# Converting the second layer's other half of the weights beside that layer instead of ahead of it, and rounding g on ScalarE

## The chip, the core and the metric

The kernel runs on one core of a Trainium2 chip. A core has a matrix engine (TensorE, PE in the rows), a vector engine (VectorE, DVE), an activation engine (ScalarE, ACT), a general engine (GpSimd, POOL) and a queue engine (SyncE, SP) that issues all of this kernel's transfers between memory (DRAM) and the on-chip buffer. The metric is the device time of one execution in microseconds (us). TensorE has two clock levels, 1.2 and 2.4 GHz; the profile tells which share of full speed was granted.

## The reference

Attention with a memory term gives x of 2304 tokens by 512. Two feed-forward layers follow, each with a hidden width of 2048 and an activation of its own:

```python
def _moe_ref(x, w_in, w_out):
    h = x @ w_in                      # (2304,512) @ (512,2048)
    g = h * np.cos(h)
    return g @ w_out                  # (2304,2048) @ (2048,512)

def _moe2_ref(x, w_in, w_out):
    h = x @ w_in
    sp = log1p(exp(min(h, 20)))       # softplus
    g = h * np.tanh(sp)               # "mish"
    return g @ w_out
```

All weights arrive as 64-bit floats, 8 bytes a number. The kernel has to turn them into 32-bit numbers itself, and it splits every matmul operand into a rounded part (H) and a remainder (L), so that each product is made of three matmuls: H with H, H with L, L with H.

## The kernel before, in words

Four stretches follow each other. **Stage A** is attention over 16 (batch, head pair) steps, with the first half of the first layer (hidden columns 0 to 1023, called `m1`) woven in. **Stage B** is what is left of `m1`, while the weights of the first layer's second half are converted. **Stage C** is the first layer's second half (`m2`): for each block of 512 tokens eight units, a unit being one group of 128 hidden columns. **Stage D** is the whole second layer (`m3`), sixteen units a block, the first eight with the weights `w_c` (first half), the other eight with `w_d` (second half).

A unit has two steps. `first` (L445) is 12 matmuls of the token block with `w_in` into a PSUM tile `h`; `second` (L503 in stages B and C, L512 in D) is 12 matmuls of g with `w_out` into `y`. The loop in `ffn` takes units in pairs: `first` of two units, then `second` of the two units before them. Between the two steps the other engines make g. In stage C (`elem_cos`): ScalarE turns h into a whole number of turns (L392), VectorE subtracts these (L393), ScalarE takes a sine over both units of the pair at once (L397), VectorE multiplies by h (L400), which is the last reader of h; then `split` rounds g (L113 to L117, on the engine that the table `TURNS` names) and subtracts the rounded part (L417, on GpSimd in stage C). In stage D (`elem_mish`): one ScalarE instruction (L409), a rounding on ScalarE, a subtraction in turn on VectorE and GpSimd.

A piece of weights (512 KB of 64-bit numbers, 128 x 512 of them; 16 pieces a half) goes through `to_f32`: a load into one of two buffers `wst` (L123), a rescaling on GpSimd (L117), one step on ScalarE (L126), three on VectorE (L127, L128, L131). `load_half` then rounds it (L113 on ScalarE or L117 on GpSimd, in turn) and subtracts (L161, VectorE or GpSimd, in turn).

In stage C of the kernel before, the 16 pieces of `w_c` go through this whole path, and then 16 pieces of `w_d` through `to_f32` alone (`convert_ahead`), and are stored to a scratch tensor `w2s` in DRAM. In stage D `from_scratch` reads them back and only the rounding and the subtraction are left to do.

The order of instructions on each engine is fixed when the program is built: a scheduler takes the instructions by their place in the program text and by a timeline of its own, and gives each buffer out again when its last reader is done. `tc.issue_after(x)` puts what follows on the engine of x behind x. On the chip each engine, and the SP queue, runs its list strictly in that order; an instruction that waits holds up all that stand behind it. `BUFS` says how many buffers a name has; `h` is a PSUM tile of one bank, `y` takes four banks.

Of the kernel before, what the change touches and what calls it, by code (L numbers as in the profile page):

```python
# [9 lines left out]
F32 = mybir.dt.float32  # L10
F32R = mybir.dt.float32r
I32 = mybir.dt.int32
# [6 lines left out]
TWO_PI = 2.0 * math.pi  # L19
BIG = 8.0e9  # L20
BUFS = dict(
    mb=2, raw=3, aD=4, kh=3, kl=3, qs=2, vt=2, qt=1, ph=2, den=2, mo=4, xH=1, xL=3, sm=7, mn=2, at=8, aT=7, u=2, e=3, g=4, h=3, y=4, xb=3, yp=3, yh=2, yl=2, wg=2, wst=2, S=6, T=8,
)
RES = 2
TOUCH = 1
# [6 lines left out]

TURNS = dict(
    sc0="p", ql0="vp", kh0="a", kl0="vp", qh0="a", aT0="a",
    sc="p", ql="vp", kh="p", kl="ppv", ws="p", w0l="pv", w1l="vp", w2l="vp", w3l="vp", gl="p", gh="v", mh="a",
    wh="ap", aT="av", yl="p", ml="vp", y0="v", y1="a", qh="a", aD="v",
)

# [5 lines left out]
def attention_moe_moe_kernel(  # L44
# [14 lines left out]
    nc = tc.nc  # L59
    P = 128  # L60
    B, NP, _, S = kT.shape
# [4 lines left out]
    TB = 256  # L66
# [43 lines left out]
    def scaled(kind, dst, src, scale=1.0, first=False):  # L110
        eng = turn_of(kind, first)
        if eng is nc.scalar:
            eng.activation(dst, src, AF.Copy, scale=scale)  # L113
        elif scale == 1.0 and eng is nc.vector:
            eng.tensor_copy(dst, src)  # L115
        else:
            eng.tensor_scalar(dst, src, scale, 1.0, ALU.mult, ALU.mult)  # L117
# [16 lines left out]
    def weight_pieces(win, wout, half, tl):  # L134

        f0 = half * FH + tl * 2 * P
        wi = win.bitcast(I32).rearrange("(c p) (f two) -> p c f two", p=P, two=2)
        for c in range(0, NC, 2):
            yield wi[:, c:c + 2, f0:f0 + 2 * P, :]
        wo = wout.bitcast(I32).rearrange("(f p) (e two) -> p f e two", p=P, two=2)  # L140
        for f in range(f0 // P, f0 // P + 2):
            yield wo[:, f]
# [22 lines left out]
    def from_double(win, wout, half):  # L165
# [1 line left out]
            for src in weight_pieces(win, wout, half, tl):  # L167
                yield to_f32(src)
        return f

    w2s = tc.dram_tile([NTL * 4, P, SM], F32, name="w2s")

    def convert_ahead():
        for tl in range(NTL):
            for n, src in enumerate(weight_pieces(w2i, w2o, 1, tl)):
                t = wk.tile([P, SM], I32, tag="wg", name="wg", bufs=BUFS["wg"])
                nc.sync.dma_start(w2s[4 * tl + n], to_f32(src, t))
                yield 0

    def from_scratch(tl):  # L180
        for n in range(0, 4, 2):
            t = wk.tile([P, 2, SM], F32, tag="u", name="wt", bufs=BUFS["u"])
            nc.sync.dma_start(t, w2s[4 * tl + n:4 * tl + n + 2].rearrange("n p f -> p n f"))
            yield t[:, 0]
            yield t[:, 1]

    def drain(g):
        for _ in g:
            pass
# [190 lines left out]
    last_sin = [None]  # L380
    marks = {}

    def elem_cos():

        state = []

        def f(h, last):
            if not state:
                state.append(wk.tile([P, 2, SM], F32, tag="u", name="u", bufs=BUFS["u"]))
            u2 = state[0]  # L390
            u = u2[:, len(state) - 1]
            nc.scalar.activation(u.bitcast(I32), h, AF.Copy, scale=INV2PI, bias=0.25)  # L392
            nc.vector.scalar_tensor_tensor(u, u.bitcast(I32), -TWO_PI, h, ALU.mult, ALU.add)  # L393
            state.append(h)
            if len(state) < 3:
                return []
            last_sin[0] = nc.scalar.activation(u2, u2, AF.Sin, bias=c_hpi).ins  # L397
            out = []
            for i in range(2):
                nc.vector.tensor_tensor(u2[:, i], state[1 + i], u2[:, i], ALU.mult)  # L400
                out.append(split(u2[:, i], "gl"))
            state.clear()
            return out
        return f

    def elem_mish():
        def f(h, last):
            e = wk.tile([P, SM], F32, tag="e", name="e", bufs=BUFS["e"])
            nc.scalar.activation(e, h, AF.Mish)  # L409
            return [split(e, "ml")]  # L410
        return f

    def split(g, kind):
        gg = wk.tile([P, 2, SM], F32R, tag="g", name="g", bufs=BUFS["g"])
        gH, gL = gg[:, 0], gg[:, 1]
        scaled("gh" if kind == "gl" else "mh", gH, g)
        turn_of(kind).tensor_tensor(gL, g, gH.bitcast(F32), ALU.subtract)  # L417
        return gH, gL

# [146 lines left out]
    def psum(name):  # L566
# [6 lines left out]
    w1p = ctx.enter_context(tc.tile_pool(name="w1p"))  # L573
    m_pools = [psum("psM")]
    at = attention(ap, [ps_a])
    m1 = ffn(m_pools, seq1, {0: w_a}, elem_cos(), load_block(xsH, xsL, True, TB), mm2_t, fin_partial,
             lambda blk: sum(blk) <= stored[0] * S)
    k_done = 0
    pieces = [0]
# [28 lines left out]
        drain(gb)  # L608
    b_pools = [psum("psB")]
    w_c, gc = load_half(w0p, "w2", from_double(w2i, w2o, 0), "w2l")  # L610
    ge = convert_ahead()
    m2 = ffn(b_pools, seq2, {1: w_b}, elem_cos(), load_block(xsH, xsL, True), mm2_t, fin_full)
    with tc.issue_after(marks["sp"]):
        for i, _ in enumerate(m2):
            if i % 2 and next(gc, 1):
                next(ge, None)
    drain(gc)
    drain(ge)
    w_d, gd = load_half(w1p, "w3", from_scratch, "w3l")
    with tc.issue_after(last_sin[0]):  # L620
        table = nc.scalar.preload_act_table_set("mish").ins
    m3 = ffn(b_pools, seq3, {0: w_c, 1: w_d}, elem_mish(), load_block(ysH, ysL, False), mm2_n, fin_out)
# [70 lines left out]
```

## Time and profile before

| | |
|---|---|
| median of 3 runs | 1109.83 us (1108.22 to 1111.08) |
| the profiled execution | 1113.66 us |
| its span, first to last instruction | 1111.9 us |
| TensorE busy | 1061.8 us, 95% |
| VectorE, ScalarE, GpSimd busy | 531.1, 450.9, 430.6 us |
| mean granted TensorE clock | 0.975 |

The profiled execution is 1.8 us longer than its span, and 3.8 us (0.3%) above the median of the runs. "Busy" for TensorE includes the time for which a matmul was held, and the ends of matmuls are modelled, so the starts of matmuls and the waits in front of them say more than the share. In the rows, L445 is line 445 of the kernel above; PE is the matmul, PEld the load of weights into the array that goes ahead of it; "x24" is 24 instructions; `u`, `e` and `g` are the tiles between `first` and `second`.

### The profile page before, as it was taken

Reading aid. Unit: us, or ns where it says so; the run is one execution under the profiler, and the core shown is the slowest. Engines: PE = TensorE matmul, PEld = TensorE weight load, DVE = VectorE, ACT = ScalarE, POOL = GpSimd, SP = SyncE. Lnnn points to the kernel's source line nnn. Section 1 sums busy time; section 2 is a strip of 40 time slices with the busy share of each in tenths; the row PEclk is TensorE's granted clock in tenths of the full one; section 3 lists DMA queues with packets and bytes.
Section 4 is the critical chain, followed back from the end, with each engine's and each line's share of the span. In section 5 each row is a group of like instructions: output and inputs, shape, how many; then the busy total and the mean of one; then the engine's idle time right before and its main releaser. Section 6 shows DMA issues by size and latency. Waiting matters only on the chain.

```text
span 1111.9 us, 17626 instructions
## 1 busy us (share of the span) xinstructions
PE 1061.8 (95%) x6672; PEld 903.1 (81%) x6672; DVE 531.1 (48%) x1282; ACT 450.9 (41%) x911; POOL 430.6 (39%) x454
## 2 busy tenths in 40 slices
PE   6988999999999999999988799999999999999998
PEld 5766788888888899987766578988888888888897
DVE  7989776557565558665777776520000000000000
ACT  6776475545454534343434333331222232131221
POOL 6987463416152334455556444670101010111100
PEclk8989799999999999999999989999999999999999
DMA  6555541414121274324565765730210210110010
GB/s 230 187 191 161 163 137 47 149 57 139 56 84 49 64 268 152 115 95 152 195 225 165 243 217 194 246 124 1 76 39 0 77 38 1 57 38 1 19 39 19
DMA packets 70853, 125.43 MB, mean 113 GB/s; under 512 B 6000, under 2 KB 25456, under 8 KB 70768
## 3 DMA queue, kind: packets, MB, share of 16 engines
q1 hardware_dynamic: 70768, 124.30, 33.8%
q8 instruction: 53, 0.87, 0.3%
q14 instruction: 32, 0.26, 0.1%
HBM read 91.77 MB, written 32.51 MB: 112 GB/s over the span
## 4 chain that ended last, share of the span: by engine, by line
PE 65%; DVE 12%; DMA 9%; ACT 6%; POOL 4%; issue 4%; SPq 0%; POOLq 0%; ACTq 0%; DVEq 0%
PE h L445 27%; PE y L512 18%; PE y L503 9%; DMA wst<-in_w2i_dram 4%; PE o L349 3%; PE tp L322 3%; PE sp L262 3%; DVE wst L127 2%; DMA wst<-in_w1i_dram 2%; DVE wst L131 2%; DVE wst L128 1%; ACT wst L126 1%; DMA wst<-in_w2o_dram 1%; DMA wst<-in_w1o_dram 1%; PE o L338 1%
## 5 line engine op out<-in xcount | busy, mean ns | idle before, releaser
L445 PE MATMUL h<-xbH,w 128*128 128x256 f32 (+1 forms) x1536 | 400.8, 341 | 15.8 <-DVE u L400 14.3
L445 PEld LDWEIGHTS h<-xbH,w 128*128 128x128 f32 x1536 | 268.9, 191 | 54.4 <-DVE u L400 18.7
L445 PE MATMUL h<-xbL,w 128*128 128x256 f32 (+1 forms) x768 | 259.8, 338 | 0.0
L503 PE MATMUL y<-g,w 128*128 128x256 f32 (+1 forms) x1344 | 227.5, 322 | 5.7 <-POOL g L417 3.9
L503 PEld LDWEIGHTS y<-g,w 128*128 128x128 f32 x1344 | 194.8, 195 | 30.7 <-POOL g L417 8.1
L512 PE MATMUL y<-w,g 128*128 128x512 f32 x864 | 201.8, 389 | 0.0
L512 PEld LDWEIGHTS y<-w,g 128*128 128x128 f32 x864 | 161.9, 188 | 33.4
L417 DVE TENSOR_TENSOR g<-e,g 128x512 fp32r<-128x512 f32 x36 | 25.6, 711 | 333.9 <-ACT g L113 333.9
L417 POOL TENSOR_TENSOR g<-e,g 128x512 fp32r<-128x512 f32 x36 | 47.0, 1305 | 313.5 <-ACT g L113 313.5
L445 PEld LDWEIGHTS h<-xbL,w 128*128 128x128 f32 x768 | 146.5, 191 | 15.1 <-issue 0.2
L409 ACT ACTIVATE e<-h 128x512 f32<-128x512 f32 x72 | 43.0, 597 | 252.1 <-PE h L445 252.1
L290 POOL TENSOR_SCALAR at<-at,sm,omg 128x128 f32<-128x128 f32 (+2 forms) x144 | 108.7, 766 | 86.6 <-DVE sm L288 51.3
L417 POOL TENSOR_TENSOR g<-u,g 128x512 fp32r<-128x512 f32 x72 | 97.9, 1373 | 88.4 <-DVE g L115 81.6
L126 ACT ACTIVATE wst<-wst,c_seven 128x512 int32<-128x512 uint32 x64 | 49.2, 769 | 110.5 <-DMA wst<-in_w2o_dram 36.8
L267 ACT ACTIVATE at<-at,mn 128x128 f32<-128x128 f32 (+3 forms) x128 | 71.0, 556 | 31.3 <-DVE mn L264 29.0
L117 POOL TENSOR_SCALAR wst<-wst 128x512 f32<-128x512 f32 x64 | 46.0, 719 | 82.8 <-DMA wst<-in_w2o_dram 21.3
L127 DVE SCALAR_TENSOR_TENSOR wst<-wst 128x512 int32<-128x512 int32 x64 | 56.5, 883 | 43.8 <-POOL wst L117 30.3
L322 PE MATMUL tp<-ident,at 128*128 128x128 f32 x384 | 67.3, 295 | 7.3 <-DVE xL L354 3.7
L349 PE MATMUL o<-aT,vt 128*64 128x128 f32 (+1 forms) x896 | 65.3, 277 | 0.0
L393 DVE SCALAR_TENSOR_TENSOR u<-u,h 128x512 f32<-128x512 int32 x72 | 48.9, 681 | 34.3 <-ACT u L392 34.2
L264 DVE CUSTOM_DVE_ANT_0 at<-sp,mask 128x128 f32<-128x128 f32 (+3 forms) x128 | 59.0, 481 | 9.3 <-PE sp L262 8.8
L322 PEld LDWEIGHTS tp<-ident,at 128*128 128x128 f32 x384 | 44.7, 147 | 20.0 <-POOL at L290 10.4
(98 smaller groups left out, 1239.5 us busy)
## 6 DMA issues: line engine op xcount, KB each, us to landing
wst<-in_w1i_dram SPq DMA_DIRECT2D x16, 512.0 KB, 3.7
wst<-in_w1o_dram SPq DMA_DIRECT2D x16, 512.0 KB, 4.3
wst<-in_w2i_dram SPq DMA_DIRECT2D x16, 512.0 KB, 4.3
wst<-in_w2o_dram SPq DMA_DIRECT2D x16, 512.0 KB, 4.9
qd<-in_qT_dram SPq DMA_DIRECT2D x16, 320.0 KB, 3.2
vt<-in_vn_dram SPq DMA_DIRECT2D x16, 320.0 KB, 3.3
xbH<-xsH SPq DMA_DIRECT2D x20, 256.0 KB, 4.5
xbL<-xsL SPq DMA_DIRECT2D x20, 256.0 KB, 4.5
```

The lines of the kernel that those rows point to most:

```text
L126: nc.scalar.activation(lo, lo.bitcast(U32), AF.Relu, scale=-(2.0 ** -29), bias=c_seven)
L127: nc.vector.scalar_tensor_tensor(lo, hi, 3, lo, ALU.logical_shift_left, ALU.bitwise_or)
L264: nc.vector.tensor_tensor_reduce(at[:, :N], sp[:, :N], mask[:, SM - q0:SM - q0 + N], SSC, 3.0e38, ALU.add, ALU.min, mn[:, j:j + 1])
L267: marks["act"] = nc.scalar.activation(at[:, :N], at[:, :N], AF.Exp, bias=mn[:, j:j + 1], scale=-1.0, accum_out=sm[:, j:j + 1]).ins
L290: turn_of("sc", b == 0).tensor_scalar(at[:, :N], at[:, :N], sm[:, j:j + 1], gates[j], ALU.mult, ALU.mult)
L322: nc.tensor.transpose(tp[:, c:c + P], at[:, c:c + P], ident)
L349: marks["pe"] = nc.tensor.matmul(o[j * D:(j + 1) * D, :n], st["vt"][:kk, c, j * D:(j + 1) * D], a, start=False, stop=c == i, skip_group_ch ...
L393: nc.vector.scalar_tensor_tensor(u, u.bitcast(I32), -TWO_PI, h, ALU.mult, ALU.add)
L417: turn_of(kind).tensor_tensor(gL, g, gH.bitcast(F32), ALU.subtract)
L445: nc.tensor.matmul(h[:, a * T:(a + 1) * T], w_[:, c, f0:f0 + P], x_[c], start=m == 0, stop=m == 3 * NC - 1)
L503: nc.tensor.matmul(y[e // per][:, cols], w_[:, f, es], g_, start=fst and m == 0 and e % per == 0, stop=lst and m == 2, skip_group_check=True)
L512: nc.tensor.matmul(y[t], g_[:, tsl], w_[:, f, :], start=fst and m == 0, stop=lst and m == 2, skip_group_check=True)
```

## The change

`convert_ahead`, `from_scratch`, the scratch tensor `w2s` and its buffers `wg` are gone. `w_d` is loaded with `from_double`, as the other three halves are, so its 16 pieces go through the whole path of `to_f32`, rounding and subtraction while stage D runs. Stage C converts `w_c` alone, one piece every fourth step of the unit loop in the program text where it was every second. In stage C the rounding of g moves from VectorE to ScalarE (`bh="a"`; stages A and B keep `gh="v"`). `h` gets a fourth buffer.

```diff
-    mb=2, ..., g=4, h=3, y=4, ..., wg=2, wst=2, S=6, T=8,
+    mb=2, ..., g=4, h=4, y=4, ..., wst=2, S=6, T=8,
...
-    ..., gl="p", gh="v", mh="a",
+    ..., gl="p", gh="v", bh="a", mh="a",
...
-    w2s = tc.dram_tile([NTL * 4, P, SM], F32, name="w2s")
-    def convert_ahead():
-        for tl in range(NTL):
-            for n, src in enumerate(weight_pieces(w2i, w2o, 1, tl)):
-                t = wk.tile([P, SM], I32, tag="wg", name="wg", bufs=BUFS["wg"])
-                nc.sync.dma_start(w2s[4 * tl + n], to_f32(src, t))
-                yield 0
-    def from_scratch(tl):
-        for n in range(0, 4, 2):
-            t = wk.tile([P, 2, SM], F32, tag="u", name="wt", bufs=BUFS["u"])
-            nc.sync.dma_start(t, w2s[4 * tl + n:4 * tl + n + 2].rearrange("n p f -> p n f"))
-            yield t[:, 0]
-            yield t[:, 1]
...
-    def elem_cos():
+    def elem_cos(cast):
...
-                out.append(split(u2[:, i], "gl"))
+                out.append(split(u2[:, i], cast, "gl"))
...
-            return [split(e, "ml")]
+            return [split(e, "mh", "ml")]
-    def split(g, kind):
+    def split(g, cast, kind):
...
-        scaled("gh" if kind == "gl" else "mh", gH, g)
+        scaled(cast, gH, g)
...
-    m1 = ffn(m_pools, seq1, {0: w_a}, elem_cos(), ...
+    m1 = ffn(m_pools, seq1, {0: w_a}, elem_cos("gh"), ...
...
-    ge = convert_ahead()
-    m2 = ffn(b_pools, seq2, {1: w_b}, elem_cos(), load_block(xsH, xsL, True), mm2_t, fin_full)
+    m2 = ffn(b_pools, seq2, {1: w_b}, elem_cos("bh"), load_block(xsH, xsL, True), mm2_t, fin_full)
     with tc.issue_after(marks["sp"]):
         for i, _ in enumerate(m2):
-            if i % 2 and next(gc, 1):
-                next(ge, None)
+            if i % 4 == 1:
+                next(gc, None)
     drain(gc)
-    drain(ge)
-    w_d, gd = load_half(w1p, "w3", from_scratch, "w3l")
+    w_d, gd = load_half(w1p, "w3", from_double(w2i, w2o, 1), "w3l")
```

Up to the start of stage C every engine's order is the same. The places that matter after it are these. The line numbers of the changed kernel are 16 lower from `from_scratch` on (L417 is L401, L540 is L524, L392 is L376, L397 is L381, L409 is L393, L537 is L521, L621 is L603).

**GpSimd in the later part of stage C.** `wst` is a weight piece, `g<-u` the subtraction of stage C, `yl` that of the result y. Before:

```order
L417 TENSOR_TENSOR g<-u,g 128x512 x2
L117 TENSOR_SCALAR wst<-wst 128x512 x3
L417 TENSOR_TENSOR g<-u,g 128x512 x2
L117 TENSOR_SCALAR wst<-wst 128x512 x2
L417 TENSOR_TENSOR g<-u,g 128x512 x2
L117 TENSOR_SCALAR wst<-wst 128x512 x4
L417 TENSOR_TENSOR g<-u,g 128x512
L540 TENSOR_TENSOR yl<-yp,yh 128x512
```

In the changed program, from the last piece of `w_c` (`w_6532`) to the first of `w_d`:

```order
L161 TENSOR_TENSOR w_6532<-wst,w_6531 128x512
L117 TENSOR_SCALAR wst<-wst 128x512 x2
L401 TENSOR_TENSOR g<-u,g 128x512 x2
L524 TENSOR_TENSOR yl<-yp,yh 128x512 x4
L401 TENSOR_TENSOR g<-u,g 128x512 x8
L524 TENSOR_TENSOR yl<-yp,yh 128x512 x4
L401 TENSOR_TENSOR g<-u,g 128x512 x8
L524 TENSOR_TENSOR yl<-yp,yh 128x512 x4
L401 TENSOR_TENSOR g<-u,g 128x512 x2
L117 TENSOR_SCALAR w_8145<-wst 128x512
```

The pieces between the g of this stretch are gone but for the two that are rescaled early (the second row): they are the first two of `w_d`, loaded into the free `wst` buffers, and the rest of their way follows in stage D.

**ScalarE where stage C ends.** `u<-u,c_hpi` is the last sine of stage C, ACT_TABLE_LOAD brings the table for mish, `e<-h` is mish. Before:

```order
L397 ACTIVATE u<-u,c_hpi 128x1024
L621 ACT_TABLE_LOAD
L113 ACTIVATE w_8290<-wt 128x512
L113 ACTIVATE w_8292<-wt 128x512
L113 ACTIVATE w_8294<-wt 128x512
L537 ACTIVATE yh<-yp 128x512
L409 ACTIVATE e<-h 128x512
```

In the changed program:

```order
L381 ACTIVATE u<-u,c_hpi 128x1024
L603 ACT_TABLE_LOAD
L126 ACTIVATE wst<-wst,c_seven 128x512 x2
L113 ACTIVATE g<-u 128x512 x2
L113 ACTIVATE w_8145<-wst 128x512
L393 ACTIVATE e<-h 128x512
L113 ACTIVATE g<-e 128x512
L126 ACTIVATE wst<-wst,c_seven 128x512 x2
L113 ACTIVATE w_8147<-wst 128x512
```

The rounding of stage C's last two g now stands behind the table load and two conversion steps, and conversion steps of `w_d` stand between the mish of the first units.

**GpSimd in stage D, where the last pieces of `w_d` are made.** `w_82..`/`w_81..` are the parts of `w_d`. Before, with `wt` the piece read back from scratch:

```order
L417 TENSOR_TENSOR g<-e,g 128x512
L161 TENSOR_TENSOR w_8299<-wt,w_8298 128x512
L117 TENSOR_SCALAR w_8300<-wt 128x512
L161 TENSOR_TENSOR w_8301<-wt,w_8300 128x512
L117 TENSOR_SCALAR w_8302<-wt 128x512
L161 TENSOR_TENSOR w_8303<-wt,w_8302 128x512
L117 TENSOR_SCALAR w_8304<-wt 128x512
L161 TENSOR_TENSOR w_8305<-wt,w_8304 128x512
L417 TENSOR_TENSOR g<-e,g 128x512 x34
```

In the changed program, the same place:

```order
L401 TENSOR_TENSOR g<-e,g 128x512
L117 TENSOR_SCALAR w_8155<-wst 128x512
L117 TENSOR_SCALAR wst<-wst 128x512
L161 TENSOR_TENSOR w_8156<-wst,w_8155 128x512
L117 TENSOR_SCALAR wst<-wst 128x512 x2
L117 TENSOR_SCALAR w_8157<-wst 128x512
L161 TENSOR_TENSOR w_8158<-wst,w_8157 128x512
L401 TENSOR_TENSOR g<-e,g 128x512
L117 TENSOR_SCALAR wst<-wst 128x512
L117 TENSOR_SCALAR w_8159<-wst 128x512
L161 TENSOR_TENSOR w_8160<-wst,w_8159 128x512
L401 TENSOR_TENSOR g<-e,g 128x512 x30
```

Two of GpSimd's g of stage D stood ahead of the last part of `w_d` before; in the changed program six do. The g in the middle of the last fence belongs to the twelfth unit of stage D and stands behind the rescaling of the first piece of the eighth and last pair of pieces (the second of the "x2").

## Rows read from the trace of the kernel before

**Rows 1.** The page: busy time and share; granted clock in 40 slices, in tenths.
```profile
PE 1061.8 (95%) x6672; PEld 903.1 (81%) x6672; DVE 531.1 (48%) x1282; ACT 450.9 (41%) x911; POOL 430.6 (39%) x454
...
PEclk8989799999999999999999989999999999999999
```

**Rows 2.** Stretches from:to us, length; busy of PE, PEld, DVE, ACT, POOL; clock, DMA share, GB/s.
```profile
483.00:600.00 117.00, 107.56 (x483) 85.50 (x483) 80.72 (x135) 42.83 (x62) 64.80 (x60) 1.00 0.49 161
600.00:720.00 120.00, 109.74 (x553) 91.73 (x552) 82.98 (x113) 40.78 (x57) 59.84 (x51) 0.97 0.68 229
720.00:1112.00 392.00, 388.30 (x1805) 325.12 (x1803) 31.46 (x44) 102.69 (x170) 64.46 (x51) 1.00 0.11 38
```

**Rows 3.** Timeline of TensorE: start us, us, engine, line, what.
```profile
483.42 0.40 PE L445 MATMUL h<-xbH,w 128*128 128x512 f32 x1
...
720.28 0.63 PE L445 MATMUL h<-xbH,w 128*128 128x512 f32 x2
```

**Rows 4.** Chain of waits in 483:720: start us, us, what.
```profile
640.70 8.33 PE h L445 x24
...
675.82 5.44 PE h L445 x24
...
686.70 5.75 PE h L445 x48
```

**Rows 5.** Waits in 483:720: who for whom, us in total, times, longest.
```profile
ACT wst L126 <- DMA wst<-in_w2o_dram: 36.8, 12, 7.4
...
ACT wst L126 <- DMA wst<-in_w2i_dram: 32.1, 14, 5.0
...
PEld h L445 <- DVE u L400: 18.7, 10, 5.9
...
PEld y L503 <- POOL g L417: 7.0, 9, 1.5
...
PEld y L503 <- DVE g L115: 2.0, 2, 1.5
```

**Rows 6.** Chain of waits in 523:548: one loop of a weight buffer.
```profile
535.71 3.38 DMA wst<-in_w2o_dram
...
539.16 0.76 ACT wst L126
539.92 0.49 ACT u L392
...
542.59 0.69 DVE wst L127
543.28 0.68 DVE wst L128 x2
543.95 0.61 DVE wst L131
...
544.64 0.66 POOL w L117
...
545.37 1.65 POOL w L161
...
547.04 3.62 DMA wst<-in_w2i_dram
```

**Rows 7.** Groups in 483:600: busy us, mean ns | idle before.
```profile
L131 DVE TENSOR_TENSOR wst<-wst 128x512 int32<-128x512 int32 x19 | 15.7, 825 | 0.1
...
L115 DVE CAST g<-u 128x512 fp32r<-128x512 f32 x20 | 8.2, 443 | 0.0
```

**Rows 8.** The same groups' view in 600:720.
```profile
L131 DVE TENSOR_TENSOR wg<-wst 128x512 int32<-128x512 int32 x15 | 16.4, 1093 | 1.5 <-POOL g L417 1.2
```

**Rows 9.** The same view in 709:820, the start of stage D.
```profile
L417 POOL TENSOR_TENSOR g<-e,g 128x512 fp32r<-128x512 f32 x10 | 13.5, 1346 | 62.9 <-ACT g L113 62.9
```

**Rows 10.** Timeline where stage C ends, ScalarE and TensorE.
```profile
707.29 1.28 ACT L621 ACT_TABLE_LOAD   x1
...
709.27 0.40 PE L445 MATMUL h<-xbH,w 128*128 128x512 f32 x1
```

More of the change, by code (lines that the diff above doesn't have):

```diff
@@ L21 @@
 BUFS = dict(
-    mb=2, raw=3, aD=4, kh=3, kl=3, qs=2, vt=2, qt=1, ph=2, den=2, mo=4, xH=1, xL=3, sm=7, mn=2, at=8, aT=7, u=2, e=3, g=4, h=3, y=4, xb=3, yp=3, yh=2, yl=2, wg=2, wst=2, S=6, T=8,
+    mb=2, raw=3, aD=4, kh=3, kl=3, qs=2, vt=2, qt=1, ph=2, den=2, mo=4, xH=1, xL=3, sm=7, mn=2, at=8, aT=7, u=2, e=3, g=4, h=4, y=4, xb=3, yp=3, yh=2, yl=2, wst=2, S=6, T=8,
 )
@@ L34 @@
     sc0="p", ql0="vp", kh0="a", kl0="vp", qh0="a", aT0="a",
-    sc="p", ql="vp", kh="p", kl="ppv", ws="p", w0l="pv", w1l="vp", w2l="vp", w3l="vp", gl="p", gh="v", mh="a",
+    sc="p", ql="vp", kh="p", kl="ppv", ws="p", w0l="pv", w1l="vp", w2l="vp", w3l="vp", gl="p", gh="v", bh="a", mh="a",
     wh="ap", aT="av", yl="p", ml="vp", y0="v", y1="a", qh="a", aD="v",
@@ L575, in attention_moe_moe_kernel @@
     at = attention(ap, [ps_a])
-    m1 = ffn(m_pools, seq1, {0: w_a}, elem_cos(), load_block(xsH, xsL, True, TB), mm2_t, fin_partial,
+    m1 = ffn(m_pools, seq1, {0: w_a}, elem_cos("gh"), load_block(xsH, xsL, True, TB), mm2_t, fin_partial,
              lambda blk: sum(blk) <= stored[0] * S)
```

## The prediction

> **What bounds the kernel now.** I read the page first: TensorE is busy for 95% of the span, the other engines for half of it or less [rows 1], so a change pays only where TensorE is held. The view by stretches comes next. From 720 us on TensorE is busy for 388.3 of 392 us at full clock, and the others are nearly idle: stage D is matmul-bound and has nothing to give, only to lose. In stage C the two stretches leave 9.4 and 10.3 us idle, with VectorE at some 70% [rows 2]; since held matmuls count as busy, I work the loss out from starts.
>
> Stage C's first matmul starts at 483.42 us; its last ends where the next L445 starts, at 720.28 us [rows 3]: 236.9 us. Unhindered, 24 matmuls of 512 columns take 5.44 us and 48 of 256 columns 5.75 us [rows 4]. Stage C has four blocks of four pairs, each pair 48 matmuls (10.88 us), and a last block of two pairs of 96 matmuls (11.5 us): 174.1 + 23.0 us. Inside the same span lie the last 48 matmuls of m1 (5.8 us) and 23 of stage D's, taken early (5.2 us). That is 208.1 us of work, so **28.8 us of holding**. The waits of the span name it: 18.7 us the loading of weights for `first` waits for L400, 7.0 us that of `second` for L417, 2.0 us for the rounding L115 [rows 5]; the rest is small, but for 2.9 us of half clock (below).
>
> Why L400? It is the last reader of h. With three h, the second unit of a pair takes the tile that the first unit of the pair before gives back, so PE is held whenever the chain L392, L393, L397, L400 is late; and it is late because a piece of weights stands in front of it. ScalarE waits 36.8 and 32.1 us for loads of weights at L126 [rows 5], with L392 of the next h queued behind. One `wst` buffer goes round in 11.3 us (535.71 to 547.04): load 3.38, L126 0.76, then L392 0.49 in between, L127 to L131 1.98, rounding 0.66, subtraction 1.65, and waits [rows 6]. A pair of units needs 10.88 us. So in stage C the weight loop, not the matmuls, sets the pace.
>
> **The change, part by part.** *Removed from stage C:* 16 pieces of `convert_ahead`, their 48 VectorE, 16 ScalarE and 16 GpSimd steps, and their stores. They stand in the later stretch, whose idle time is 10.3 us, plus 2.9 us in which 24 matmuls took 8.33 instead of 5.44 us after a hold of over 5 us [rows 2, 4]: 13.2 us that go with them. What is late next there? Only the cosine chain is left, with less than 6 us of work on any engine in a 10.88 us pair, so I expect nothing but the hand-over of `y` from block to block.
>
> *The fourth h and the rounding on ScalarE, beside `w_c`:* the 16 pieces of `w_c` stay in stage C's earlier stretch, and the loop with them. Taking the casts off VectorE removes 0.44 us each, two a pair [rows 7], and puts two ScalarE roundings at its end, behind the weight's own. The fourth h moves the wait for L400 one pair back: 10.88 us of slack instead of half of that. Bounds: all of that stretch's holding goes (15.6 us, which is 28.8 less 13.2) but for 2.0 us, or, if the loop stays at 11.3 against 10.88 us with g's wait taking over from h's, 0.5 us a pair over eight pairs and the hand-overs stay, some 8 us. I take 2 us for the loop, 2.0 us for the last rounding of m1 (L115 stays on VectorE there), and 2 us for hand-overs of y: **6 us stay of 28.8, a gain of 22.8 us**.
>
> *Where stage C ends:* the last two roundings of g stand behind the table load and two L126: 1.28 + 2 x 0.76 = 2.8 us [rows 6, 10]. PE has 21 early matmuls of stage D (4.8 us) and 48 of the pair before (5.8 us) to run, against some 9 us of sine, table, rounding and subtraction. Cost 0; up to 2 us if the sine is late.
>
> *Added to stage D:* 16 pieces through the whole path. As work it is little; as a queue it matters. All times from here are from the table load, T. The two first pieces are already loaded, and their L126 follow the load; the second is through L131 at about T + 5.2, waits on GpSimd for two old g, is rounded and subtracted (0.66 + 1.65) by T + 10.3, and its buffer's next load lands at T + 14. The next round has two subtractions of `yl` ahead on GpSimd, each like a g of 1.35 us [rows 9]: T + 14 + 10.8 + 2.7 = T + 27.5 for the second piece of pair 3. The loop here: 11.3 us as in stage C is the upper bound, since there is less beside it; without the cosine steps in it (0.49 of L392 and as much waiting) it is 10.3 us. I take **10.8 us**. Pair 7 lands at T + 27.5 + 4 x 10.8 = T + 70.7; the first piece of pair 8 is issued some 2.4 us later, when VectorE has freed its buffer, and lands 4 us after that: T + 77.1. On GpSimd the g of the twelfth unit stands behind this piece's L117, and the rounding and subtraction of pair 7's second piece: + 0.66 + 0.66 + 1.65 + 1.35 = T + 81.4.
>
> PE wants it when? Stage D begins 2 us after T [rows 10]. Up to the twelfth unit's `second` there stand the first four units and stage C's last 48 (16.6 us), ten groups of 24 (54.4 us) and the eleventh unit's `second` (2.7 us): T + 75.7, or a microsecond later if stage C, less loaded, ends more closely. So PE is held for **5 us**; 5 us more for each microsecond of a longer loop, 0 at 9.8 us. The parts of `w_d` themselves are in time (the last `w_in` part by T + 80, due at T + 78.5 plus the hold), and the second half of the next x, queued on SP behind the last piece, by T + 85, due near T + 89.
>
> *Sum:* 1113.66 - 22.8 + 5 = 1095.9 us for the profiled execution, which is 3.8 us above the median of the runs: **1092 us**.
>
> The granted clock fell after the one long hold of before [rows 4]. The Trainium skill's page "TensorE: Matmul & The Clock Gate" ("What's actually happening") says that the slow level is the default, which activity lifts; by it a hold of 5 us in stage D would cost the same 2.9 us again, and the sum would be 1095. The holds of half that length in the earlier stretch show no fall, so I leave it to the range.
>
> **Rivals.** *No hold in stage D.* If the loop is under 10 us, or the scheduler's spacing leaves more room than I count, only some 4 us of stage C's holding remain: 1109.8 - 25 = 1085. For it: mish takes fewer steps than the cosine. Against: 10.3 us is already made of bare durations.
>
> *The loop stays at 11.3 us everywhere.* Then the earlier stretch keeps 12 us of its holding and loses 13.2 + 3.6 of the rest, and stage D is held for 8 us, with the clock's 2.9: a net gain of 6 us at best, 1104 to 1108. For it: rows 6 show just this loop; against: half of it is waiting for the cosine chain.
>
> *Slower: stage D's loop at 13.8 us or more.* One mechanism: GpSimd's and VectorE's two-input steps holding each other up. L131 takes 0.825 us on average in the earlier stretch and 1.093 in the later [rows 7, 8]. If each loop loses over 3 us in this way, the g of the twelfth unit is 15 us later than I say, the hold is 20 us and the clock falls: the gain is gone at 13.8 us a loop; at 14.5 us it is 1109.8 - 22.8 + 23.5 + 2.9 = 1113. Against: the means above give 0.3 us a step, under 1 us a loop.
> The Trainium skill's page "SBUF — State Buffer" ("Who interferes with whom") makes this exclusive: a VectorE step with two SBUF inputs and a GpSimd step that reads SBUF do not share, the later is blocked for all of the other. By it the two GpSimd subtractions of a loop (1.65 and 1.35 us) would make it 13.3 us and the hold 17.5 us, with the clock 20.4: 1107, no change. The rows' means lie well below that, as the two seldom meet; hence a small chance.
>
> *The change does not do what it says:* the wait for L400 only becomes a wait for g. Then 15 us of holding stay, 13.8 go, and stage D costs 8 us and the clock's 2.9: 1107.
>
> **How the numbers follow.** My forecast (stage D held for 2 to 8 us, 4 to 9 us left in stage C: 1086 to 1098) has 0.55, no hold in stage D 0.20, the loop at 11.3 us 0.12, blocked engines without loss or a wait turned into a wait for g 0.08, slower 0.05. Runs of this kernel can be told apart from about 0.3%, 3.3 us. Faster by more: the first two, most of the third: 0.85; within: 0.10; slower: 0.05. The range takes in most of the second and third: 1083 to 1106.
>
> **What would show it.** In the profile after: stage C's 24-matmul groups at 5.44 us from its middle on, no stores to scratch, waits of PE for L384 (the old L400) near 0 in total; stage C shorter by about 23 us; a clean start of stage D, then one hold near 75 us after the table load, named after GpSimd's g (L401), and a `wst` loop of 10.3 to 11.3 us there. Wrong would be: a hold in stage D of more than 10 us or none; holds for g in the middle of stage C; any change before 480 us.

## The result and the profile after

The changed kernel takes 1097.14 us (median of 4 runs, 1096.84 to 1098.41) against 1109.82 us of the kernel before beside it: ratio 0.9889, interval 0.9872 to 0.9906. It is faster by 12.7 us; the forecast was 1092 us with a range of 1083 to 1106. The profiled execution took 1098.41 us where the sum made for it said 1095.9.

The page of the changed kernel, to be held against [rows 1], and three stretches, to be held against [rows 2] (columns as there):

```profile
PE 1056.2 (96%) x6672; PEld 903.1 (82%) x6672; DVE 517.7 (47%) x1246; ACT 472.7 (43%) x947; POOL 428.4 (39%) x454
...
PEclk8998799999999999999999999999999999999999
```

```profile
484.00:600.00 116.00, 107.72 (x481) 86.83 (x480) 78.81 (x115) 54.32 (x81) 69.70 (x64) 0.99 0.49 166
600.00:705.00 105.00, 105.00 (x553) 90.77 (x552) 36.21 (x53) 42.07 (x60) 40.91 (x33) 1.00 0.43 143
705.00:1096.00 391.00, 388.05 (x1805) 325.04 (x1803) 63.07 (x86) 111.55 (x182) 74.25 (x65) 1.00 0.14 48
```

The earlier stretch of stage C has hardly moved: TensorE was idle for 9.4 of 117 us and is idle for 8.3 of 116. The later stretch had 10.3 us of idle time and has none, and it is over after 105 us instead of 120. Stage D takes twice VectorE's work (31.5 to 63.1 us) and does not get longer. TensorE's timeline gives the ends of stage C, as [rows 3] did; the ScalarE row is the table load T (707.29 us in [rows 10]):

```profile
484.08 0.40 PE L429 MATMUL h<-xbH,w 128*128 128x512 f32 x1
...
705.49 0.63 PE L429 MATMUL h<-xbH,w 128*128 128x512 f32 x2
```

```profile
691.28 1.28 ACT L603 ACT_TABLE_LOAD   x1
```

Stage C: 221.4 us where it was 236.9, so 15.5 us shorter; stage D to the end of the span: 391.1 against 391.6 us. The waits of TensorE's weight loading in 484:706 (who for whom, us in total, times, longest) answer to the last three rows of [rows 5]:

```profile
PEld h L429 <- DVE u L384: 6.9, 4, 2.7
PEld h L429 <- DMA xbH<-xsH: 2.4, 1, 2.4
PEld y L487 <- POOL g L401: 1.4, 3, 0.6
PEld y L487 <- DVE g L115: 1.3, 1, 1.3
```

The wait for the last reader of h (L384, the old L400) fell from 18.7 to 6.9 us, that for g from 7.0 to 1.4. Most of this fall belongs to the later stretch; up to 600 us the kernel before shows:

```profile
PEld h L445 <- DVE u L400: 11.4, 8, 2.9
```

Its wait for g there was 1.2 us, so in the earlier stretch the gain is 4.5 us on h, and 2.4 us of waits for a load of x are new, which were not followed up. All of the waits after the change lie before 590 us. One of them, in the timeline:

```profile
511.23 1.29 DVE L384 TENSOR_TENSOR u<-h,u 128x512 f32<-128x512 f32 x2 [0.61 <-ACT u L381]
...
511.98 0.50 PE L429 MATMUL h<-xbH,w 128*128 128x512 f32 x1 [1.44 <-DVE u L384]
```

```profile
500.96 5.89 DMA wst<-in_w2o_dram
510.05 1.16 ACT u L381
511.23 1.29 DVE u L384 x2
...
660.58 5.44 PE h L429 x24
```

The second fence is the chain of waits (start us, us, what): at 511 us it runs from a load of weights through sine and product to the held matmul; from 585 us on it is TensorE alone, 24 matmuls in 5.44 us, the unhindered figure of [rows 4].

In the tables below, **holds** are worked out from the starts of matmuls: the step from one to the next, less 0.227 us (512 columns) or 0.12 us (256 columns), summed where over 0.25 us. Matmuls at half clock fall below that and are given apart where they matter. Before: 10.8 us of holds in stage C up to 600 us, 11.9 from there to T, 0 in stage D; after: 9.3, 0, 0.

### The profile page after: what moved, and what is told of

Read it like the earlier page. It is cut to its first block, busy times and chain, and to the rows that moved or that the text cites. A ratio compares the mean times of both kernels' runs of the same rounds, so it can differ in the third digit from the quotient of the medians.

```text
span 1096.6 us, 17569 instructions
## 1 busy us (share of the span) xinstructions
PE 1056.2 (96%) x6672; PEld 903.1 (82%) x6672; DVE 517.7 (47%) x1246; ACT 472.7 (43%) x947; POOL 428.4 (39%) x454
## 4 chain that ended last, share of the span: by engine, by line
PE 70%; DVE 11%; DMA 7%; ACT 5%; POOL 4%; issue 3%; SPq 0%; ACTq 0%; POOLq 0%; DVEq 0%
PE h L429 29%; PE y L496 18%; PE y L487 12%; PE o L333 3%; PE tp L306 3%; PE sp L246 3%; DMA wst<-in_w1i_dram 2%; DVE wst L127 2%; DMA wst<-in_w1o_dram 2%; DVE wst L131 2%; DMA wst<-in_w2o_dram 1%; PE o L322 1%; DVE wst L128 1%; DMA wst<-in_w2i_dram 1%; DVE w L161 1%
## 5 line engine op out<-in xcount | busy, mean ns | idle before, releaser
L487 PE MATMUL y<-g,w 128*128 128x256 f32 (+1 forms) x1344 | 224.8, 321 | 2.1 <-POOL g L401 1.2
L401 DVE TENSOR_TENSOR g<-e,g 128x512 fp32r<-128x512 f32 x36 | 25.3, 702 | 288.9 <-ACT g L113 258.3
L429 PEld LDWEIGHTS h<-xbL,w 128*128 128x128 f32 x768 | 146.1, 190 | 15.9 <-DMA xbL<-xsL 0.8
L401 POOL TENSOR_TENSOR g<-e,g 128x512 fp32r<-128x512 f32 x36 | 47.7, 1325 | 276.4 <-ACT g L113 276.4
L401 POOL TENSOR_TENSOR g<-u,g 128x512 fp32r<-128x512 f32 x72 | 95.9, 1347 | 122.0 <-ACT g L113 64.7
L393 ACT ACTIVATE e<-h 128x512 f32<-128x512 f32 x72 | 42.8, 594 | 216.6 <-PE h L429 216.2
L127 DVE SCALAR_TENSOR_TENSOR wst<-wst 128x512 int32<-128x512 int32 x64 | 54.2, 847 | 68.1 <-POOL wst L117 34.4
L376 ACT ACTIVATE u<-h 128x512 int32<-128x512 f32 x72 | 41.8, 591 | 80.9 <-PE h L429 72.3
```

The costliest lines, as they stand in the source:

```text
L127: nc.vector.scalar_tensor_tensor(lo, hi, 3, lo, ALU.logical_shift_left, ALU.bitwise_or)
L429: nc.tensor.matmul(h[:, a * T:(a + 1) * T], w_[:, c, f0:f0 + P], x_[c], start=m == 0, stop=m == 3 * NC - 1)
L487: nc.tensor.matmul(y[e // per][:, cols], w_[:, f, es], g_, start=fst and m == 0 and e % per == 0, stop=lst and m == 2, skip_group_check=True)
```

## The experiments

Ratios are to the kernel before, run on the same chip beside each kernel (1109.82 us beside the changed kernel; 1111.22, 1115.85 and 1112.25 us in the three sets of experiments, so medians of different sets are not compared). The expectations give times for a kernel before of about 1110 us; where a set's kernel before is slower, as in the second, a range is held against the ratio.

| kernel | median us | ratio, interval | holds: C to 600, 600 to T, D |
|---|---|---|---|
| changed | 1097.14 | 0.9889 (0.9872 to 0.9906) | 9.3, 0, 0 |
| weights only | 1102.26 | 0.9923 (0.9896 to 0.9949) | 12.3, 0, 4.5 |
| three h | 1097.60 | 0.9879 (0.9848 to 0.9910) | 12.0, 0, 0 |
| one tile of four banks | 1228.36 | 1.1054 (1.1021 to 1.1086) | 44.2, 52.9, 9.1 |
| paced | 1086.49 | 0.9779 (0.9752 to 0.9807) | 1.2, 0, 0 |
| rounding on VectorE | 1105.62 | 0.9922 (0.9897 to 0.9947) | 10.5, 2.6, 4.6 |
| scratch kept | 1113.56 | 0.9989 (0.9963 to 1.0015) | 10.8, 9.3, 0 |
| four tiles | 1102.17 | 0.9883 (0.9847 to 0.9918) | 10.6, 0, 0.9 |
| before, paced | 1118.94 | 1.0036 (1.0005 to 1.0067) | 11.6, 15.9, 0 |
| loaded twice | 1118.76 | 1.0057 (1.0026 to 1.0088) | 10.6, 1.0, 18.0 |
| paced alone | 1091.38 | 0.9828 (0.9793 to 0.9863) | 1.0, 0, 2.8 |

### Which part of the change does it

**Weights only**: the changed kernel without the fourth h and with g rounded on VectorE.

```diff
-    ..., g=4, h=4, ...
+    ..., g=4, h=3, ...
-    ..., bh="a", mh="a",
+    ..., bh="v", mh="a",
```

> Only the weights are moved: the second half of the second layer's weights is converted in stage D; g is rounded on VectorE in stage C as before, and h keeps three buffers. Theory 1 (all of the gain is the 16 pieces taken out of stage C's later stretch, 15 us of holding; the other two edits give nothing): 1095 to 1099 us, with holds of TensorE of about 12 us before 600 us and none after it. Theory 2 (the fourth h and the rounding on ScalarE carry a part of the gain): 1101 us or more, with L400's wait larger in the earlier stretch than the 6.3 us seen after the change.

**Three h**: the changed kernel with `h=3` alone.

> The changed kernel with three buffers of h again. Theory 1 (the packer gave the eighth PSUM bank to only one h in ten, so the fourth buffer hardly acts): within 2 us of the changed kernel, 1095 to 1099 us, holds for the last reader of h in the earlier stretch as after the change, 6 to 9 us. Theory 2 (the fourth buffer acts): 3 us or more slower, 1100 us or more.

**Rounding on VectorE**: the changed kernel with `bh="v"` alone.

> The changed kernel with one edit undone: g of the first layer's second half is rounded on VectorE again (the fourth h and the conversion beside the first half stay). Theory 1, from the run with the weights alone (1102.26 us) and its three-h twin (1097.60 us): the rounding's engine does nothing for the first layer's second half; the sequence of the second layer comes out otherwise and its weights come late for the units 8 to 11. It expects 1100 to 1103 us, TensorE held 12 to 13 us between 484 and 600 us as in the changed kernel, none between 600 us and the table load, and 3 to 6 us in the second layer, 60 to 80 us after the table load. Theory 2: VectorE, relieved of 36 casts, answers the cosines sooner: the same 1100 to 1103 us, but 4 us or more of new holds before the table load (over 17 us in all there), and none in the second layer. Theory 3: the rounding is worth nothing, 1096 to 1098 us, and the difference of the two runs was chance.

**Scratch kept**: the kernel before with `h=4` and `bh="a"`; the 16 pieces still go through DRAM.

> The kernel before with the fourth h and the rounding on ScalarE alone: the 16 pieces still go through DRAM and 32 pieces are converted in the first layer's second half. Theory 1: the holds after 600 us come from those 16 pieces and the other two edits give nothing by themselves. It expects 1106 to 1111 us, 10 us or more of holds between 600 us and the table load, and none in the second layer. Theory 2: relieved queues and a fourth h take holds away in both stretches whatever the pieces do: 1095 to 1101 us, under 6 us of holds after 600 us.

The weights-only run came out where its Theory 2 had it, at 1102 us: the other edits carry a part. In stage C, though, it is as Theory 1 said, with 12.3 us of holds up to 600 us and none from there to T; what it lacks lies in stage D. Moving the 16 pieces alone gives 0.9923; the other two edits without it give 0.9989, which is no change that can be told. The fourth h is worth nothing with either rounding (0.9889 against 0.9879, 0.9922 against 0.9923). In the changed program nearly every unit's h is placed in one of three banks; of the fourth buffer one h per block makes use. With the rounding on VectorE the packing is another, the first half of stage C goes round in four banks, and the waits change their name. TensorE's largest wait in 484:706 with the weights only (three h), then with the rounding on VectorE (four):

```profile
PEld h L429 <- DVE u L384: 12.5, 7, 2.9
```

```profile
PEld y L487 <- POOL g L401: 13.8, 11, 2.5
```

With four h in use no wait for the product is left, and there is as much waiting for g. The rounding on ScalarE is worth 0.3 to 0.4% with either number of h (0.9879 against 0.9923, 0.9889 against 0.9922; the intervals overlap at their ends, the holds in stage D, 0 against 4.5 and 4.6 us, point the same way), but not where I had put it. TensorE's two largest waits in the kernel with the rounding on VectorE, 690:790, all in stage D:

```profile
PEld y L496 <- POOL g L401: 2.9, 2, 2.2
PEld y L496 <- DVE g L401: 2.7, 2, 2.0
```

The changed kernel has no wait of that engine there. Timeline of TensorE with the weights only (T is at 690.50 us):

```profile
755.18 3.03 PE L496 MATMUL y<-w,g 128*128 128x512 f32 x12 [0.30 <-DVE g L401]
760.02 2.56 PE L496 MATMUL y<-w,g 128*128 128x512 f32 x10 [1.81 <-POOL g L401]
...
770.02 2.33 PE L496 MATMUL y<-w,g 128*128 128x512 f32 x9 [1.55 <-DVE g L401]
```

This is a hold in stage D of nearly the predicted size (4.5 us), at T + 64 to T + 80, but in several pieces, for the g of the ninth, tenth and eleventh units, where the prediction had one hold for the twelfth. Stage D has the same instructions in both kernels; their sequence differs. In the traces the sequence on ScalarE, GpSimd and VectorE after T is one and the same in every kernel with the rounding on ScalarE and `w_d` converted in stage D (changed, three h, paced, four tiles), and another one in the three with it on VectorE (weights only, rounding on VectorE, paced alone). ScalarE at the mish of the ninth unit, with the weights only (T + 62), and in the changed kernel (T + 54):

```profile
752.19 0.76 ACT L126 ACTIVATE wst<-wst,c_seven 128x512 int32<-128x512 uint32 x1 [4.31 <-DMA wst<-in_w2o_dram]
752.85 0.57 ACT L393 ACTIVATE e<-h 128x512 f32<-128x512 f32 x1
```

```profile
744.59 0.76 ACT L126 ACTIVATE wst<-wst,c_seven 128x512 int32<-128x512 uint32 x1 [3.95 <-DMA wst<-in_w2o_dram]
745.25 0.58 ACT L393 ACTIVATE e<-h 128x512 f32<-128x512 f32 x1
```

In both it stands behind a conversion step that waits some 4 us for a load; with the weights only that is the second piece of the sixth pair, in the changed kernel the first. So Theory 1 of the rounding run is right on stage D. It is not right that stage C is untouched: 2.6 us of holds for g appear after 600 us. Whether that is VectorE's load, the other packing of h or again a sequence wasn't separated. With three h the same edit leaves stage C alone (12.3 and 12.0 us). The three-h run is its Theory 1 in time; its holds in the earlier stretch (12.0 us, 10.9 of them waits for the product) are above the 6 to 9 us expected.

The scratch run is its Theory 1: holds of 9.3 us after 600 us, a little under the 10 that the theory asked for, and by the ratio 1109 us (its median lies above the range, as that set's kernel before does above 1110).

### Why the earlier stretch keeps its holds

**One tile of four banks**: h of stages C and D is written in turn into the four banks of one PSUM tile, so that a pair needs the banks of the pair before the last.

```diff
+    ring = b_pools[0].tile([P, 4, SM], F32, tag="h", name="hr", bufs=1)
...
-            h = pools[k // 2 % len(pools)].tile([P, SM], F32, tag="h", ...)
+            h = ring[:, k % 4]
```

> The changed kernel with h in stages C and D taken in turn from one tile of four PSUM banks, so that a unit takes the bank of the unit four before it, whatever the packer does. Theory 1 (holds for the last reader of h in stage C come from reuse of a bank given up by the pair just before): those holds, 6.3 us and 1.6 us of half clock, fall below 2 us; 1089 to 1093 us, unless the two transfers that held TensorE near 585 us are held longer. Theory 2 (the loop of the weight buffers sets the pace of stage C's earlier stretch, whatever h has): the holds turn into holds for g (L401) of the same total; 1095 to 1099 us.

It is 117 us slower than the kernel before, and so decides between neither theory. Its timeline:

```profile
641.49 1.29 DVE L384 TENSOR_TENSOR u<-hr,u 128x512 f32<-128x512 f32 x2 [1.22 <-ACT u L381]
642.83 0.79 PE L432 MATMUL hr<-xbH,w 128*128 128x512 f32 x1 [3.91 <-DVE u L384]
...
643.85 1.05 PE L432 MATMUL hr<-xbH,w 128*128 128x512 f32 x2
```

Every pair waits for the product of the pair just before it, although that one reads the other two banks: the order is kept for the tile as a whole. And each such hold, of about 4 to 9 us, is followed by 7 to 13 matmuls at half clock (two matmuls begin 0.43 us apart here, 0.227 us elsewhere), another 1.4 to 2.6 us.

**Four tiles**: the same with four tiles of one bank.

```diff
+    ring = [b_pools[0].tile([P, SM], F32, tag=f"h{n}", name=f"h{n}", bufs=1) for n in range(4)]
...
+            h = ring[k % 4]
```

> The changed kernel with the first matmul's outputs of the first layer's second half and of the second layer in four tiles of their own, one bank each, written in turn, in place of four buffers of one tag that are placed in three banks for nearly all units. A pair then waits for the sines of the pair before the last, not of the last. Theory 1: the 5.8 us of holds on the sine product (VectorE's u) come from the banks, so a real fourth bank takes them and the half-clock matmuls after them away: 1088 to 1093 us, no hold on that product over 0.5 us. Theory 2: the pairs are paced by the weight loop of 12 us that stands in the same queues; the matmuls run further ahead and then wait for g, or the holds stay: 1095 to 1099 us, 5 us or more of holds between 500 and 590 us, on g or on u. Unlike the run with one tile of four banks, no pair should wait for the pair just before it (4.07 us each there).

TensorE's waits, 484:700, the two largest:

```profile
PEld y L490 <- POOL g L401: 7.6, 7, 2.4
PEld h L432 <- DMA xbH<-xsH: 2.3, 1, 2.3
```

The waits for the product are gone, and 7.6 us of waits for g stand in their place; the time is the changed kernel's (0.9883 against 0.9889). Theory 2: more banks let `first` run ahead, but g comes when it comes, as with the rounding on VectorE above. The bank was where the wait showed, not its cause.

**Paced**: in the changed kernel the engine work of each piece in stage C is put behind the last sines already issued on ScalarE.

```diff
             if i % 4 == 1:
-                next(gc, None)
+                with tc.issue_after(last_sin[0]):
+                    next(gc, None)
```

> The changed kernel with each piece of w_c in stage C put behind the last sine traced so far on ScalarE, so that the pieces spread over the whole of stage C (one piece a pair) instead of two a pair in its earlier part. Theory 2 (the loop of the weight buffers against the pace of the pairs makes the holds): with one piece a pair there is half of the queue in front of the cosine chain, holds in stage C fall from 12.9 to 5 us or less, 1088 to 1092 us. Theory 1 (bank reuse by itself): holds for the last reader of h stay at 5 us or more and spread over all of stage C, 1094 us or more.

Its stretch 484:590:

```profile
484.00:590.00 106.00, 104.91 (x485) 87.25 (x484) 69.46 (x93) 48.89 (x72) 59.27 (x50) 1.00 0.44 146
```

TensorE's waits in stage C, the larger of the two that are left (the other is 0.5 us for g):

```profile
PEld y L487 <- DVE g L115: 1.5, 1, 1.5
```

TensorE is idle for 1.1 of 106 us, the waits for the product are gone, and the kernel is the fastest of all, 24.7 us under the kernel before. That is Theory 2, and 1.5 us better than its range. The third step of a piece (L131) in 500:590, before, after, paced (busy us, mean ns):

```profile
L131 DVE TENSOR_TENSOR wst<-wst 128x512 int32<-128x512 int32 x14 | 12.0, 854 | 0.1
```

```profile
L131 DVE TENSOR_TENSOR wst<-wst 128x512 int32<-128x512 int32 x15 | 13.6, 919 | 0.2
```

```profile
L131 DVE TENSOR_TENSOR wst<-wst 128x512 int32<-128x512 int32 x9 | 13.0, 1447 | 0.3
```

The changed program text hands out one piece a pair, but the scheduler starts a piece as soon as one of the two buffers is free, so the chip sees 15 pieces in 90 us, as before, nearly two in each pair of 10.88 us; then from 593 us on none until T. Paced, it is 9 in that stretch, and the last of the 16 ends at 664.6 us.

**Before, paced**: is it the place behind the sines, or the number? The kernel before, its 32 pieces and scratch kept, with the same constraint. (The expectation speaks of 40 pairs; stage C has 18.)

```diff
             if i % 2:
-                if next(gc, 1):
-                    next(ge, None)
+                with tc.issue_after(last_sin[0]):
+                    if next(gc, 1):
+                        next(ge, None)
```

> The kernel before, all its 32 pieces and the scratch in DRAM kept, with one edit: the ScalarE work of each piece in the first layer's second half is put behind the last sines already issued, as in the paced run of the changed kernel (1086.49 us). Theory 1: the holds come from pieces that stand in the queues ahead of a pair's cosine chain, not from how many there are: paced, the 32 pieces fit between the 40 pairs and the time is 1083 to 1090 us, with under 5 us of holds between 484 us and the table load. Theory 2: the amount of conversion is what the stretch can't carry: 1098 to 1112 us, with 10 us or more of holds, or pieces left over at the table load that the second layer waits for.

```profile
PEld h L445 <- DVE u L400: 12.7, 7, 3.5
PEld h L445 <- DMA xbH<-xsH: 9.2, 2, 4.9
```

Theory 2, and by the ratio 1114 us, a little above its range. With two pieces a pair the place behind the sines gains nothing, even in the first hundred us (11.6 us of holds against 10.8 without it; 13 pieces in 500:590 where it was 14); later the loads of x come late as well. So the place alone does not free the earlier stretch: it is held while it converts nearly two pieces a pair, and free at one piece a pair behind the sines, which is all it needs. Half the rate without the constraint on the place was not tried, so it is not shown that the rate alone would do.

**Paced alone**: the paced kernel with `h=3` and `bh="v"`.

> The paced kernel (1086.49 us) with the fourth h and the rounding on ScalarE undone: only the pieces moved to the second layer, and the remaining ones put behind the last sines. Theory 1: with the pieces out of the cosine chain's way neither edit has anything left to gain in the first layer's second half; the second layer keeps the sequence in which its weights come late: under 3 us of holds between 484 us and the table load, 3 to 6 us of holds in the second layer, 1088 to 1093 us. Theory 2: as Theory 1, and the second layer comes out in the better sequence: 1085 to 1088 us and no hold there. Theory 3: the rounding on ScalarE relieves VectorE in the first layer's second half even so: 5 us or more of holds before the table load, 1090 to 1097 us.

```profile
PEld y L496 <- POOL g L401: 2.6, 2, 2.2
```

Theory 1: 1.0 us of holds in stage C without either edit, and the hold in stage D again, 2.8 us and 2.1 us of half clock. That hold is about what lies between this and the paced kernel (0.0049, some 5.4 us).

### What stage D hangs on

**Loaded twice**: each piece of `w_d` is loaded twice into its buffer, which lengthens the loop and adds no arithmetic.

```diff
         nc.sync.dma_start(st, src)
+        if again:
+            nc.sync.dma_start(st, src)
```

> The changed kernel with one thing added: each piece of the second half of the second layer's weights is loaded twice into the same buffer, so that a buffer's loop in the second layer grows by about one landing (3.6 us, from 9.9 to 13.5). Theory 1: that loop decides whether the second layer waits. In the changed kernel the eleventh unit's g is ready 0.1 us after its matmuls could start, without any margin; six to seven loops, each 3.6 us longer, make the first piece of pair 8 land some 96 us after the table load in place of 72, and TensorE waits 15 to 27 us for g between 50 and 120 us after the table load: 1112 to 1124 us. Theory 2: the conversion's arithmetic on three engines sets the loop and the second load is hidden in part: 3 to 12 us of holds, 1100 to 1109 us. Theory 3: the loop is not what the second layer waits for: 1096 to 1099 us.

```profile
PEld y L498 <- ACT g L113: 11.5, 3, 7.1
```

```profile
775.00:795.00 20.00, 12.09 (x42) 9.13 (x43) 7.42 (x11) 4.57 (x7) 7.09 (x8) 0.74 0.53 165
```

Theory 1 (its "eleventh unit", counted from 0, is the twelfth in this text): a loop of 14.6 us (six loops, 698.16 to 785.70 us), 18.0 us of holds and 4.0 us of half clock in stage D (granted clock 0.74 in the stretch shown), 18.7 us slower than the changed kernel by the ratios (0.0168 of 1111). The wait is named after g's rounding on ScalarE, since it stands there behind a conversion step whose piece is late.

## Why the prediction was right and where it was not

**The later stretch** (13.2 us to go with the 16 pieces): right, and a little more. 11.9 us of holds and 3.1 us of slower matmuls, 15.0 us, became 0, and nothing new came late there. With the pieces their stores to the scratch tensor went too; which of the two held TensorE was not separated.

**The earlier stretch** (6 us to stay): this step failed. 9.3 us of holds and 3.1 us of slower matmuls stay, 12.4 of the 13.0 that the same count gives for before. The prediction let the fourth h give 10.88 us more of slack. It is hardly used (three h is as fast), and where it is (four tiles, rounding on VectorE) the wait becomes one for g: the fourth rival, but in this stretch alone. The working had the right sentence, that the weight loop sets the pace, and then counted only 2 us for it. The loop from load to load is 11.6 us in the changed kernel (499.79 to 546.09, four loops) where a pair needs 10.88, and both buffers go round in it, two pieces a pair. I took the program text's every fourth step for the pace on the chip.

**The end of stage C** at no cost: right; no matmul is held between 590 us and stage D.

**Stage D held for 5 us**: there was no hold. The path that the prediction followed is the right one; two of its terms were too long. Issues of the loads of `w_d` on the SP queue in the changed kernel:

```profile
700.11 1.51 SPq L123 DMA_DIRECT2D wst<-in_w2o_dram  x2
...
716.13 0.37 SPq L123 DMA_DIRECT2D wst<-in_w2i_dram  x1
...
750.86 6.10 SPq L123 DMA_DIRECT2D wst<-in_w2i_dram  x2
759.74 7.17 SPq L123 DMA_DIRECT2D wst<-in_w2o_dram  x2
```

A row of two begins with the one buffer's load and holds the other's too. The first term is the loop of the buffer that the prediction followed: the second piece of pair 3 (issued at 716.13 us) lands at T + 28.4 (predicted 27.5) and that of pair 7 at T + 69.1 (70.7), so 10.2 us a loop where I had taken 10.8. The second term is the larger: the first piece of pair 8 was to be issued 2.4 us after that landing and to land 4 us later. Its buffer goes round apart from the other (700.11 to 759.74 us, six loops of 9.94 us); the load is issued 0.6 us before pair 7's second piece has landed, and lands at T + 72.0 (predicted 77.1). From there it is as predicted, 4.7 us instead of 4.3: the twelfth unit's g is ready at T + 76.7 (81.4), and its matmuls start at T + 76.6 (due 75.7, or a microsecond later), the first of them that reads the remainder at T + 77.0: in time by next to nothing. Four tiles, with the same sequence, has a hold of 0.9 us just there. In the three kernels with g rounded on VectorE the other sequence of stage D has holds of 2.8 to 4.6 us; and a loop of 14.6 us brings 18 us of holds and 4 us of half clock (by the prediction's rule, 5 us for each microsecond of loop from 9.8 us on, 24).

**The sum.** Stage C gained 15.5 us instead of 22.8, stage D cost -0.5 instead of 5: errors of 7.3 and 5.5 us on opposite sides, which with 0.7 us by which stage C begins later leave 2.5 us in the profiled execution. As much again comes from the step to the median: the profiled execution lies 1.3 us above it, not 3.8. So 1092 us was 5.1 us short. Of the prediction's own signs, the 24-matmul groups at 5.44 us from the middle of stage C on and no change before 480 us came out; waits for L384 near 0 (6.9 us), a stage C shorter by 23 us (15.5) and a hold in stage D did not, and no hold there is among those it had called wrong. The range held because two steps failed against each other, not because each was right: that is luck. What happened is one half each of two rivals: of the second, the loop that stays at 11.3 us, its first half (12 us stay in the earlier stretch), and of the first its stage D (a loop of about 10 us, no hold).

## What to carry to other kernels

Before a wait for a buffer is cured with another buffer, look at what its last reader was waiting for: if a second chain in the same queues sets the pace, the wait moves to the next hand-over and the time stays. Where a background job may run as early as its buffers allow, look at its rate on the chip, not at the rate at which the program hands it out; here one conversion a pair behind the sines, instead of nearly two, was worth some 12 us (0.9889 to 0.9779) with the same instructions. And a stage whose margin is 0 us in one sequence is late in another: an edit in the stage before it can cost 5 us there without touching it.

## What the runs showed of the hardware

**The clock can fall after shorter holds than I assumed.** The prediction said that holds of half of 5 us show no fall. In the changed kernel one of 2.3 us does: half clock from 526.8 to 530.2 us, 1.6 us lost (granted clock 0.79 in 524:532):

```profile
525.47 0.50 PE L429 MATMUL h<-xbH,w 128*128 128x512 f32 x1 [2.28 <-DVE u L384]
...
526.50 0.47 PE L429 MATMUL h<-xbL,w 128*128 128x512 f32 x1
526.77 1.05 PE L429 MATMUL h<-xbH,w 128*128 128x512 f32 x2
```

The first matmuls after the hold still run at the upper level (2.4 GHz), the next at the lower (1.2 GHz, 0.43 us apart). The length of a hold does not decide it by itself. With the weights only, one of 1.91 us (to 584.77 us) is followed by half clock too (0.91 in 580:600), while those of 2.49 us (to 559.52 us), 1.81 and 1.55 us show none (1.00 in 555:575 and 750:775). Nor does this one in the kernel before, at a granted clock of 1.00 in 555:575, which is what the prediction had read:

```profile
561.47 0.51 PE L445 MATMUL h<-xbH,w 128*128 128x512 f32 x1 [2.49 <-DVE u L400]
```

What else decides it, these runs do not show. The Trainium skill's page "TensorE: Matmul & The Clock Gate" ("What's actually happening") has the slow level as the default, which activity lifts; these rows agree with it.

**VectorE and GpSimd do shut each other out.** Timeline of the paced kernel:

```profile
528.28 3.03 POOL L401 TENSOR_TENSOR g<-u,g 128x512 fp32r<-128x512 f32 x2 [2.32 <-ACT g L113]
528.76 1.40 DVE L128 TENSOR_SCALAR wst<-wst 128x512 int32<-128x512 int32 x1
530.19 1.66 DVE L131 TENSOR_TENSOR wst<-wst 128x512 int32<-128x512 int32 x1
```

```profile
L128 DVE TENSOR_SCALAR wst<-wst x19: 422/790/1403, 484.5 to 659.3; 128x512 int32<-128x512 int32 x19
L131 DVE TENSOR_TENSOR wst<-wst x19: 687/1657/1668, 485.2 to 660.7; 128x512 int32<-128x512 int32 x19
```

The second fence gives durations (ns; least, median, most). L131 takes 687 ns alone and 1657 beside a subtraction on GpSimd; it begins when the engine is free and ends about 0.55 us after that subtraction does. It goes the other way too: in the paced kernel a subtraction on GpSimd takes 1.30 us alone (at 491.38 us) and 1.75 when it begins during the last 0.59 us of an L131 (at 586.93 us). The one-input L128 is stopped likewise, 422 to 1403 ns. That is the lock of the page "SBUF — State Buffer" of the Trainium skill ("Who interferes with whom"), which the prediction had weighed against means of 825 and 1093 ns [rows 7, 8]; the means are mixtures of the two durations. The prediction gave it a small weight, as the two seldom meet. In stage D, of which that was said, they do not meet often; the same view of the changed kernel in 705:770:

```profile
L131 DVE TENSOR_TENSOR wst<-wst x13: 684/694/1793, 706.0 to 766.9; 128x512 int32<-128x512 int32 x13
```

In the paced kernel's stage C most of these steps are stopped (14 of the 19 take over 1 us), its mean of L131 is the worst of the three shown above, and it is the fastest kernel: where the loop has room, the stops cost TensorE nothing.
